# Turning the first two row tiles on TensorE, and a new order for every engine, in a two-layer linear-attention and SwiGLU kernel

## The chip, the cores and the metric

The kernel runs on one core of one Trainium2 chip. A core has five engines with instruction queues of their own: TensorE (PE), VectorE (DVE), ScalarE (ACT), GpSimd (POOL) and SyncE (SP), which here issues the DMA transfers. The metric is the device time of one execution, in microseconds (us).

## The reference

Two layers of two blocks each, with the same weights in both layers. The input is x with 2048 rows of 512 values; there are 32 heads of 16, and the hidden width of the gated block is 1792.

```python
def _A_ref(x, wqkv, wo):
    qkv = (x @ wqkv).reshape(B, S, 3, H, Dh).transpose(2, 0, 3, 1, 4)
    q, k, v = qkv[0], qkv[1], qkv[2]
    phi = lambda t: jnp.where(t > 0, t + 1, jnp.exp(t)) + 1e-6
    pq, pk = phi(q), phi(k)
    kv = jnp.einsum("bhsd,bhse->bhde", pk, v)
    z = jnp.einsum("bhsd->bhd", pk)
    num = jnp.einsum("bhqd,bhde->bhqe", pq, kv)
    den = jnp.einsum("bhqd,bhd->bhq", pq, z)[..., None] + 1e-6
    o = num / den
    return o.transpose(0, 2, 1, 3).reshape(B, S, D) @ wo

def _B_ref(x, w1, w3, w2):
    h = _silu(x @ w1) * (x @ w3)
    return h @ w2

x = x + _A_ref(_layernorm(x), wqkv, wo)
x = x + _B_ref(_layernorm(x), w1, w3, w2)
x = x + _A_ref(_layernorm(x), wqkv, wo)
x = x + _B_ref(_layernorm(x), w1, w3, w2)
```

## The kernel before, in words

**Precision.** A product of float32 matrices is made of float16 parts. Each operand is split into a high part (a rounded copy, by ACT, L834 for weights and L935 for normalised rows) and a low part (the rest, by DVE at L835 for weights, by POOL at L936 for rows), and `mm` (L945) runs three passes: high by high, high by low, low by high. So one product of a 128-row tile with a 512 x 512 weight is 4 x 3 = 12 matmuls of 512 columns.

**Tiles.** x is kept in SBUF as 16 row tiles of 128 rows. TensorE needs the rows of its operand turned (values on partitions): `ln_tile` (L930) normalises a tile (L922), splits it into the buffer `nat`, and has a transposing DMA transfer (L937) write the turned tile `xt`. The normalising needs mean and variance from DVE (L907, L908) and scale and offset from POOL (L915 to L919, `nb_all` last).

**Stages.** From 0 to about 13 us x and the weights of the keys come in, PE runs 32 matmuls on ones (`keep_busy`, named warm), and the largest weight is found: DVE's L787 and L803 give each partition's maximum, the small matmul `pm_k` (L806) spreads it, and DVE's L808 to L819 make the scale from it that the weight splits (L834) wait for. Then comes layer 0's attention: keys pk by row tile, their phi (L1337 to L1339), the products of keys and values kv (`gram`, L1364), then the queries, the output po and the adds to x (L1951). It is over at about 200 us, with the first MLP already mixed in. That MLP runs to about 577 us. It is written in a seven-product form (Strassen-Winograd) in half blocks of 256 columns: `mlp_group` (L2027) with DVE's block sums (L2022, L2023, L2053), and `mlp_out` (L2085; its matmuls are L2095, its adds L2144). Layer 1's attention, to about 760 us, has a seven-product form of its own, in which two row tiles are taken as a pair: `pair_rows` and `pair_turn` (L1564, L1569; sums L1573 to L1590 and the transposing transfer L1591), `products7` (L1595) with the banks ka to kc, qa to qc, whose results ACT and DVE combine (L1632, L1636), and `attention7` (L1640) with the pairs' loads `load7` (q_d and xt_d in DRAM), the phi of the queries (L1716), their division (L1730 to L1748), the products POOL rounds (L1758) and transposing transfers (L1767) ahead of the output po. Between keys and queries stand the folding of kv into the weights (L1794 to L1818). The second MLP runs to about 1140 us.

**What sets the order.** Nothing is left to a scheduler: `arrange` (L679) counts each engine's instructions in the order in which the program makes them, and pins them to the order that the table `ORDER` (L73) writes out, one list of numbers for each of PE, DVE, Activation, Pool and SP. An engine runs its list strictly in order, so an instruction that waits holds up all that stand behind it in the list. A DMA's place on SP's list sets when it can be issued.

**Names the prediction uses.** pk, kv, pq, po, kc, qa to qc, gt, ba to bc are PSUM banks by what is computed in them; `x_piece(t0, t1)` loads row tiles, `att_piece(1)` the four quarters of the keys' weights; `first_tile(t)` (L2339) makes the first turned tiles.

Of the kernel before, what the change touches and what calls it, by code (L numbers as in the profile page):

```python
# [495 lines left out]
def kernel(  # L496
# [1818 lines left out]
    def x_piece(t0, t1):  # L2315
        for t in range(t0, t1):
            nc.sync.dma_start(x_sb[:, t, :], x_rows[:, t, :])
# [120 lines left out]
```

## Time and profile before

| | |
|---|---|
| median of 3 runs | 1146.06 us (1145.27 to 1146.5) |
| the profiled execution's own time | 1146.37 us |
| its span in the profile | 1144.7 us |
| granted TensorE clock, mean | 0.999 |
| matmuls | 9108 |
| mean DMA rate | 143 GB/s |

The span runs from the first to the last instruction that the profiler recorded; what lies around it is part of the execution's time. A line of the trace has start and duration in us, the engine, the line of the source, the operation, out<-in and, in brackets, how long the engine was idle before it and what ended the idle time. Matmuls are pipelined: the recorded duration of one is longer than the distance to the next one's start.

### The profile page before, as it was taken

The page shows a single profiled execution, that of the slowest core. Times are in us where ns is not written, and L with a number is a line of the kernel's source. Part 1 is how long each engine was busy: PE and PEld are TensorE (multiplying, and loading weights), DVE is VectorE, ACT ScalarE, POOL GpSimd, SP SyncE. Part 2 cuts the span into 40 slices and gives each one's busy share as a digit, 9 for nine tenths or more (in the row PEclk, how much of TensorE's full clock was granted, in tenths as well). Part 3 has the DMA queues.
Part 4 walks back from the last instruction along what each step waited for, and adds up shares of the span by engine and source line. Part 5 has one row for each costly group of instructions (what it writes and reads, how often), then busy time and mean ns, then how long its engine had stood idle before and what let it go on. Part 6 is the DMA issues. An engine that isn't in the chain of part 4 may idle for free.

```text
span 1144.7 us, 22435 instructions
## 1 busy us (share of the span) xinstructions
PE 1126.6 (98%) x9108; PEld 887.6 (78%) x9108; DVE 853.8 (75%) x1468; ACT 656.7 (57%) x1099; POOL 422.4 (37%) x477
## 2 busy tenths in 40 slices
PE   8999999999999999999999999999999999999998
PEld 3445445888888888888885676578888888888887
DVE  6789878897888887889895478857855765455555
ACT  6687877765545545555577755676544335343432
POOL 5641796402001313334588315781153100302114
PEclk9999999999999999999999999999999999999999
DMA  9995855785662432251368955565256150202001
GB/s 271 298 268 181 211 119 114 209 243 109 244 230 97 153 148 102 85 179 65 79 169 196 248 169 127 97 152 148 70 113 257 70 207 1 84 19 93 11 19 56
DMA packets 173880, 163.46 MB, mean 143 GB/s; under 512 B 141648, under 2 KB 150096, under 8 KB 169168
## 3 DMA queue, kind: packets, MB, share of 16 engines
q1 hardware_dynamic: 173776, 162.03, 48.9%
q8 instruction: 71, 1.16, 0.4%
q14 instruction: 33, 0.27, 0.1%
HBM read 80.08 MB, written 47.32 MB: 111 GB/s over the span
## 4 chain that ended last, share of the span: by engine, by line
PE 86%; DVE 5%; ACT 3%; POOL 2%; DMA 2%; issue 1%; SPq 0%; DVEq 0%; POOLq 0%; ACTq 0%
PE bb L945 25%; PE po L2095 19%; PE bc L945 13%; PE ba L945 6%; PE gt L945 6%; PE po L945 4%; PE pk L945 3%; PE po L2115 3%; PE pq L945 3%; DMA arena<-arena 1%; PE kb L945 1%; PE qb L945 1%; DVE arena L869 1%; POOL arena L1590 1%; ACT arena L1632 1%
## 5 line engine op out<-in xcount | busy, mean ns | idle before, releaser
L945 PEld LDWEIGHTS <-arena 128*128 128x128 f16 x6648 | 645.9, 98 | 215.4 <-issue 10.4
L945 PE MATMUL bb<-arena 128*128 128x256 f16 x2688 | 351.2, 273 | 0.4 <-DMA arena<-arena 0.4
L2095 PE MATMUL po<-arena 128*128 128x256 f16 x2058 | 292.9, 273 | 0.7 <-DVE arena L2144 0.7
L2050 ACT ACTIVATE arena<-bb 128x512 f32<-128x512 f32 x196 | 115.6, 593 | 199.2 <-PE bb L945 168.2
L2095 PEld LDWEIGHTS <-arena 128*128 128x128 f16 x2058 | 201.3, 98 | 24.2 <-DVE arena L2144 1.0
L945 PE MATMUL bc<-arena 128*128 128x256 f16 x1344 | 179.7, 273 | 1.9 <-DVE arena L2053 1.9
L2053 DVE TENSOR_TENSOR arena<-arena,bc 128x512 f32<-128x512 f32 x112 | 76.6, 684 | 68.8 <-PE bc L945 33.7
L2011 DVE TENSOR_TENSOR arena<-arena 128x1280 f16<-128x1280 f32 (+1 forms) x90 | 105.4, 1174 | 28.5 <-ACT arena L2009 28.4
L2144 DVE SCALAR_TENSOR_TENSOR arena<-po,scalars,arena 128x256 f32<-128x256 f32 (+1 forms) x180 | 101.6, 585 | 30.8 <-PE po L2095 24.8
L2005 ACT ACTIVATE arena<-arena,scalars 128x512 f32<-128x512 f32 x112 | 74.5, 666 | 84.6 <-DVE arena L2053 70.7
L2009 ACT ACTIVATE arena<-arena 128x512 f16<-128x512 f32 (+1 forms) x112 | 100.6, 903 | 27.5 <-DVE arena L2006 9.7
L2006 DVE SCALAR_TENSOR_TENSOR arena<-arena,scalars 128x512 f32<-128x512 f32 x112 | 77.8, 695 | 38.1 <-ACT arena L2005 37.8
L945 PE MATMUL ba<-arena 128*128 128x256 f16 x672 | 92.3, 273 | 0.0
L945 PE MATMUL gt<-arena 128*128 128x512 f16 x384 | 89.4, 379 | 1.0 <-POOL arena L1652 1.0
L945 PE MATMUL po<-arena 128*128 128x512 f16 x384 | 86.5, 379 | 2.0 <-DMA arena<-arena 1.9
L2011 POOL TENSOR_TENSOR arena<-arena 128x512 f16<-128x512 f32 x22 | 28.2, 1280 | 125.8 <-ACT arena L2009 96.8
L2153 POOL TENSOR_TENSOR arena<-arena 128x512 f32<-128x512 f32 x27 | 37.8, 1402 | 94.5 <-DVE arena L2144 94.5
L2152 POOL TENSOR_TENSOR arena<-arena 128x512 f32<-128x512 f32 x27 | 36.8, 1362 | 65.0 <-DVE arena L2144 63.5
L869 DVE SCALAR_TENSOR_TENSOR arena<-arena,scalars 128x512 f16<-128x512 f32 (+2 forms) x74 | 59.8, 822 | 1.1 <-ACT arena L867 0.9
L922 ACT ACTIVATE arena<-arena,nb_all,rs_all 128x512 f32<-128x512 f32 x64 | 50.7, 805 | 14.2 <-POOL nb_all L919 8.9
L2021 POOL TENSOR_TENSOR arena<-arena 128x256 f32<-128x256 f32 x10 | 8.1, 814 | 133.1 <-DVE arena L2006 133.1
L867 ACT ACTIVATE arena<-arena,scalars 128x512 f16<-128x512 f32 (+2 forms) x74 | 52.1, 717 | 4.2 <-DVE scalars L819 1.8
(228 smaller groups left out, 1448.1 us busy)
## 6 DMA issues: line engine op xcount, KB each, us to landing
arena<-xb_d SPq DMA_DIRECT2D x12, 1792.0 KB, 7.1
xb_d<-arena SPq DMA_DIRECT2D x8, 1792.0 KB, 6.8
w_d<-arena SPq DMA_DIRECT2D x5, 1792.0 KB, 7.7
arena<-w_d SPq DMA_DIRECT2D x5, 1792.0 KB, 9.0
arena<-in_B_w_dram SPq DMA_DIRECT2D x8, 896.0 KB, 6.2
arena<-in_B_w_dram SPq DMA_DIRECT2D x28, 256.0 KB, 3.3
xt_d<-arena SPq DMA_DIRECT2D x8, 896.0 KB, 6.0
arena<-xt_d SPq DMA_DIRECT2D x8, 896.0 KB, 5.3
```

The source lines that it names most:

```text
L867: nc.scalar.activation(hi, src, AF.Copy, scale=scale)
L869: lambda: nc.vector.scalar_tensor_tensor(lo, src, scale, hi, OP.mult, OP.subtract)
L922: nc.scalar.activation(dst, x_sb[:, t, :], AF.Identity, scale=rs_all[:, t : t + 1], bias=nb_all[:, t : t + 1],)
L945: nc.tensor.matmul(dst, lhs(a, k), rhs(b, k), start=first and k == 0 and i == 0, stop=last and k == n - 1 and i == len(PASSES) - 1, skip_g ...
L2005: nc.scalar.activation(t, gate, AF.Silu, scale=info["u1"])
L2006: nc.vector.scalar_tensor_tensor(t, up, info["hid"], t, OP.mult, OP.mult)
L2009: nc.scalar.activation(hs[:, 0, lo:hi], t[:, lo:hi], AF.Copy)
L2011: engine.tensor_tensor(hs[:, 1, lo:hi], t[:, lo:hi], hs[:, 0, lo:hi], OP.subtract)
L2050: nc.scalar.activation(dst, bank_, AF.Copy)
L2053: nc.vector.tensor_tensor(dst, dst, bank_, OP.add)
L2095: nc.tensor.matmul(po[:, i * HALF : (i + 1) * HALF], hs[:, a, qx, cs], w2[:, b, qw, :], start=g == ends[0] and i + a + b == 0, stop=g == e ...
L2144: nc.vector.scalar_tensor_tensor(dst, src, cb, to, OP.mult, OP.add)
```

## The change

Tiles 0 and 1 are no longer turned by a transposing transfer. `first_tile` normalises them as before, and for the high and then the low part four TensorE matmuls with `ident16`, a float16 identity matrix that ACT copies out of `ident` at the start, write the turned part into a PSUM bank, from where one ACT copy moves it to `xt`. Tile 2 and all later ones still go by `ln_tile`. The program's order of loads is changed (tile 1 behind the keys' weights; a recorded handle in `x_piece` is not used by anything). PE has 16 instructions more, ACT 5 more, SP 2 fewer, DVE and POOL as many as before.

All five lists of `ORDER` are replaced. Since a list's numbers count the program's instructions, a number n of the old lists stands for the same instruction as n + 16 in PE's new list (from pm_k on), n + 5 in Activation's, n − 2 in SP's; in DVE's and Pool's it is the same.

```diff
 ORDER = {
     "PE": (
-        "0-56 69-80 57-68 93-104 81-83 90-92 84-89 117-128 114-116 108-110 141-152 105-107 "
...
-        "5365-5376 5341-5352 5419-5424 5377-5382 5395-5418 5431-5436 5425-5430 5389-5394 "
...
+        "0-20 22-31 34 21 35-37 32 38-48 33 49-72 85-96 73-84 109-120 100-102 97-99 106-108 "
...
+        "5375-5386 5339-5344 5399-5404 5435-5440 5387-5392 5357-5368 5393-5398 5411-5422 "
+        "5441-5452 5405-5410 5453-5476 5423-5434 5477-5572 5585-5596 5573-5584 5609-5620 "
...
     "DVE": (
-        "1 9-13 15 14 16-18 20-21 19 22 24 23 31 29 7 32 30 36 25 37 26-28 39-40 4 33 42 5 38 34 "
...
-        "317-318 294-296 298-300 308 302-305 349 335 321 307 306 350 311 320 319 339-340 310 322 "
...
-        "666 675 669 742 670 686 672 676 671 677-679 673 685 689 674 766 688 767 680 690 707 702 "
...
-        "959 964-965 985 968 972 970 984 973 971 969 986 988-989 992-995 991 990 987 997-998 "
...
-        "1028 1039-1040 1038 1031 1042-1046 1041 1047-1048 1057 1049-1050 1053-1054 1058 "
...
+        "294-296 298-299 770 300 302 304 308 303 289 305 349 335 321 307 306 350 319-320 311 "
...
+        "658 666 669 678 675-676 670 686 677 671 679 685 673 672 680 768 689 674 688 702 765 690 "
...
+        "980 962 964 966 968 965 985 969 972 984 970-971 973 986 992 988 993 989 994-995 990-991 "
...
+        "1030 1028 1027 1039-1040 1038 1031 1036 1042-1046 1041 1037 1049-1050 1047-1048 1057 "
...
     "Activation": (
-        "0-5 8-9 6-7 14 10 12 11 15 13 17 16 19 21 20 18 22-24 29 26-27 25 28 32 30 34-35 33 38 "
...
-        "752 722 760 751 731 759 724 732 768 727 725 733 726 761 728-730 741 737 767 736 743 739 "
...
+        "0-2 5-6 13 3-4 14 9-12 7-8 15 19 17 16 20 18 24 22 25 21 29 26 23 27-28 34 31 30 32-33 "
...
+        "724-725 720 727-728 757 756 764 736 765 737-738 729-730 766 731 746 772 747 732 748 741 "
...
     "Pool": (
...
-        "295 294 296-297 318-319 310 302 320 313 311 305 304 321 306-307 312 283 315 314 316-317 "
...
+        "272 274 265 303 293 247 273 248 276 278 277 252 249 253 255 292 279 254 267 302 266 "
...
     "SP": (
-        "0-2 4 3 5-7 25 8 11-12 9 21 18-19 22 20 23 10 26 30 36 24 27 17 28 48 31-32 13 34 54 42 "
...
-        "188 202 175 189 201 192 203-204 206 205 207 178 208-209 212 210-211 213-216 226 217 "
...
+        "0 5-6 1 3 2 4 7 9-10 20 19 17 16 23 18 21 8 24 28 22 25 15 34 26 52 29 36 40 53 32 30 27 "
...
+        "213-214 212 215 234 217-218 221-222 219 223 225-229 224 231-232 230 216 235 233 236 220 "
...
     ident = view(AT_UV + 2 * KB, F32, P)
     make_identity(nc, ident)
+    ident16 = view(AT_UV + 2 * KB + 512, F16, P)
+    nc.scalar.activation(ident16, ident, AF.Copy)
...
     def x_piece(t0, t1):
         for t in range(t0, t1):
-            nc.sync.dma_start(x_sb[:, t, :], x_rows[:, t, :])
+            last["t"] = nc.sync.dma_start(x_sb[:, t, :], x_rows[:, t, :])
...
-    x_piece(0, 2)
+    x_piece(0, 1)
     att_piece(1)
-    x_piece(2, 4)
+    x_piece(1, 4)
...
     def first_tile(t, engine=nc.gpsimd):
-        ready[0][t] = xk_ring.next(F16, 2 * NK, P)
-        ready[1][t] = ln_tile(t, ready[0][t], engine)
+        xt = ready[0][t] = xk_ring.next(F16, 2 * NK, P)
+        if t > 1:
+            ready[1][t] = ln_tile(t, xt, engine)
+            return
+        xn = f32()
+        normalise(xn, t)
+        nat = ready[1][t] = ring["nat"].next(F16, 2, D)
+
+        def turned(a):
+            turn = bank(f"turn{a}")
+            for k in range(NK):
+                at = slice(k * P, (k + 1) * P)
+                nc.tensor.matmul(turn[:, at], nat[:, a, at], ident16, start=True, stop=True)
+            flat = xt[:, a * NK : (a + 1) * NK, :].rearrange("p k n -> p (k n)")
+            nc.scalar.activation(flat, turn, AF.Copy)
+
+        nc.scalar.activation(nat[:, 0, :], xn, AF.Copy)
+        turned(0)
+        engine.tensor_tensor(nat[:, 1, :], xn, nat[:, 0, :], OP.subtract)
+        turned(1)
```

On SP's list the loads now run tile 0, 1, 2 of x, then the keys' weights, then the rest of x.

760 rows, old and new, of the table ORDER are left out of this document.

## The prediction

> **What bounds the kernel now.** I read the page's head first, to see which engine is full.
>
> ```profile
> span 1144.7 us, 22435 instructions
> PE 1126.6 (98%) x9108; PEld 887.6 (78%) x9108; DVE 853.8 (75%) x1468; ACT 656.7 (57%) x1099; POOL 422.4 (37%) x477
> PE 86%; DVE 5%; ACT 3%; POOL 2%; DMA 2%; issue 1%; SPq 0%; DVEq 0%; POOLq 0%; ACTq 0%
> ```
>
> TensorE (PE) is busy 1126.6 of 1144.7 us, so no new order can win more than the 18.1 us between them, and the ends before the first and after the last matmul come off that. The view of stretches, cut at the kernel's stages, tells where PE stands idle. The first figure of a row after the bounds is its length, the next PE's busy time.
>
> ```profile
> core 0: us, PE busy (x) PEld busy (x) DVE busy (x) ACT busy (x) POOL busy (x), PEclk, DMA share, GB/s
> 13.00:100.00 87.00, 86.06 (x399) 39.42 (x400) 72.49 (x145) 62.41 (x101) 41.05 (x89) 1.00 0.94 258
> 100.00:200.00 100.00, 97.60 (x531) 49.83 (x529) 84.84 (x167) 80.18 (x178) 69.54 (x69) 1.00 0.65 157
> 200.00:577.00 377.00, 376.04 (x3440) 336.14 (x3439) 318.62 (x545) 209.33 (x344) 104.94 (x106) 1.00 0.46 148
> 577.00:760.00 183.00, 176.05 (x1230) 117.95 (x1228) 129.25 (x216) 124.22 (x202) 105.60 (x107) 1.00 0.69 172
> 760.00:1140.00 380.00, 380.00 (x3476) 339.98 (x3475) 239.28 (x374) 174.29 (x270) 93.28 (x87) 1.00 0.27 88
> ```
>
> Idle are 0.94 + 2.40 + 0.96 + 6.95 + 0.00 = 11.25 us; layer 1's attention in pair form (577 to 760) has 6.95 of it, and the second MLP none. The list of what PE waited for (total, times, longest) names the pieces:
>
> ```profile
> PE bc L945 <- DVE arena L2053: 1.9, 1, 1.9
> PE po L945 <- DMA arena<-arena: 1.9, 1, 1.9
> PE qc L945 <- ACT arena L1632: 1.2, 1, 1.2
> PE pk L945 <- DMA arena<-arena: 1.2, 2, 1.0
> PE gt L945 <- POOL arena L1652: 1.0, 1, 1.0
> PE kc L945 <- DMA arena<-arena: 0.8, 1, 0.8
> PE po L2095 <- DVE arena L2144: 0.7, 1, 0.7
> PE qb L945 <- DVE arena L1636: 0.6, 1, 0.6
> PE pk L945 <- DVE arena L835: 0.6, 1, 0.6
> PE qa L945 <- DVE arena L1818: 0.6, 1, 0.6
> ```
>
> Most are single waits: a table that puts one operation earlier on the releasing engine removes one. A wait costs about 0.16 more than its idle, since a matmul of 512 columns is booked with 379 ns (0.38) and starts every 0.217, as (2.55 − 0.38)/10 from the row at 15.68 below shows.
>
> **The change, part by part. The start.** Its timeline (start, duration, last the idle and its releaser):
>
> ```profile
> 1.11 7.41 PE L2348 MATMUL warm<-ones 128*128 128x512 f16 x22 [1.11 <-DVE ones L708]
> 2.08 0.26 ACT masks.py:370 ACTIVATE mask<-mask 128x64 uint32<-128x64 uint32 x1
> 9.28 1.15 POOL L936 TENSOR_TENSOR arena<-arena 128x512 f16<-128x512 f32 x1 [0.21 <-ACT arena L935]
> 9.36 0.46 PE L806 MATMUL pm_k<-arena,scalars 128*128 128x128 f32 x2 [0.84 <-DVE scalars L803]
> 9.66 2.32 PE L2348 MATMUL warm<-ones 128*128 128x512 f16 x10
> 10.75 1.33 ACT L834 ACTIVATE arena<-arena,scalars 128x512 f16<-128x512 f32 x2 [1.54 <-DVE scalars L819]
> 11.64 1.23 SPq L937 DMA_TRANSPOSE arena<-arena  x1
> 12.98 2.11 PE L945 MATMUL pk<-arena 128*128 128x512 f16 x8 [1.00 <-DMA arena<-arena]
> 13.74 1.32 ACT L834 ACTIVATE arena<-arena,scalars 128x512 f16<-128x512 f32 x2
> 14.48 1.81 DVE L835 SCALAR_TENSOR_TENSOR arena<-arena,scalars 128x512 f16<-128x512 f32 x2 [1.47 <-ACT arena L834]
> 15.68 2.55 PE L945 MATMUL pk<-arena 128*128 128x512 f16 x11 [0.59 <-DVE arena L835]
> 17.09 0.67 ACT L1337 ACTIVATE arena<-pk,scalars 128x512 f32<-128x512 f32 x1
> ```
>
> *Removed*: two transposing transfers; tile 1's (issued at 11.64) releases pk at 12.98, and each kept SP's queue over 1.2 us, so tile 2's moves up. *Added*: 16 matmuls of 128 columns, four copies out of PSUM on ScalarE (ACT) and ident16's making.
>
> ```profile
> 108.82 2.03 PE kv L945 x36
> ```
>
> By this piece of the chain, 36 matmuls of 128 columns in 2.03 us, one takes 0.056, so 16 take 0.9 us. They lie in PE's idle time and between warm-ups, which only fill time, so I cost them at nothing. Without that cover they cost the 0.9.
>
> [...]
>
> Now what waits on what. In PE's new order pm_k stands behind tile 1's low-part transposes, so it starts when the low part (POOL L936, 10.43 before, some 0.07 later now) is done and turned, about 11.0 in place of 9.36. Queued behind it on PE are only ten warm-ups and the keys; DVE's scale and through it ACT's splits wait for it. From pm_k to the first weight split went 10.75 − 9.36 = 1.39; the splits (L834) start about 12.4. The new ACT table runs all four in a row, where before tile 2's normalising stood between the pairs: 12.4 + 4 × 0.66 = 15.05, as before (13.74 + 1.32 = 15.06). The last low part (L835) follows 0.8 behind, 15.85 in place of 14.48 + 1.81 = 16.29. Against that 0.44, tile 1's two PSUM copies, 0.67 each by the L1337 row, run after the splits and end near 16.4, which holds tile 1's keys about 0.15. Net gain: **0.3**. Bounds: −1.6 if both waits (1.0 and 0.6) vanish; +2.9 if all ACT's new work (4 × 0.67, and ident16's copy at about the 0.26 of the row at 2.08) goes ahead of the splits. Loads on SP's queue: tile 2 and the rest of x move ahead of the weights and put them back by less than pm_k now waits for the turning (1.6), so nothing; without that cover, one tile's issue and landing, under 1 us.
>
> **The waits later on**, each placed in the new tables against what it waited for:
>
> ```profile
> 741.16 2.61 SPq L1767 DMA_TRANSPOSE arena<-arena  x2
> 604.47 1.22 POOL L1652 COPY arena<-scalars 128x2 f16<-128x2 f16 x1
> 712.60 0.81 ACT L922 ACTIVATE arena<-arena,nb_all,rs_all 128x512 f32<-128x512 f32 x1 [2.17 <-POOL nb_all L1970]
> L2023 DVE TENSOR_TENSOR arena<-arena x39: 408/418/1484, 291.8 to 1119.4; 128x256 f32<-128x256 f32 x39
> ```
>
> - *po for the transposing transfer, 1.9.* VectorE's (DVE's) two adds of L1951 now stand behind L1716 of the last queries (positions 1036, 1037 behind 1031), so the work ahead of the transfers at 741.16 ends earlier; and PE's second twelve po matmuls (5423-5434) move behind 24 others (5453-5476), 12 × 0.217 = 2.6 us or more. Removed, 1.9 + 0.16 = 2.1.
> - *qc for L1632, 1.2.* The ACT copy queued behind L922, which waited 2.17 us for POOL; it now goes first (727 before 757). Removed, 1.4.
> - *gt for L1652, 1.0.* That POOL copy, held at 1.22 us, moves thirty places earlier. Removed, 1.2.
> - *po for L2144, 0.7.* It followed a 1.39 us instance of L2023 (row: median 0.418, most 1.484), which now comes after it. Removed, 0.8.
> - *qb for L1636*: five po matmuls move ahead: 0.6. *The second pk wait for a transfer*, 0.2: x comes earlier: 0.4.
> - *kc for a transpose, 0.8*: the ACT work ahead of it goes one place up, yet on SP's queue the load of q_d (row below) is moved from well behind to right behind it. I take half of 1.0: 0.5.
>
> Together 2.1 + 1.4 + 1.2 + 0.8 + 0.6 + 0.4 + 0.5 = **7.0** removed.
>
> ```profile
> 190.12 0.74 DVE L1951 SCALAR_TENSOR_TENSOR arena<-po,scalars,arena 128x512 f32<-128x512 f32 x1
> 681.86 1.22 DVE L1716 SCALAR_TENSOR_TENSOR arena<-arena 128x1024 f32<-128x1024 f32 x1
> arena<-q_d SPq DMA_DIRECT2D x1, 1792.0 KB, 10.8
> ```
>
> Given back, where the tables stand worse: bc's wait of 1.9 stays and gets another L1951 add ahead of its releaser, +0.7; qa's releaser L1818 changes places with its neighbour, +0.7; L1716 (1.22) goes ahead of the operation that pm waits for, of whose time PE's stock hides half, +0.6. **+2.0.** The queue also matters: q_d's load takes 10.8 us, and the last pair's transposes stand behind it, with 1.8 us to spare by the old times.
>
> Waits that only the new order makes have no row. From below: the bc, qa and kc waits left could go too, −4.3. From above: the new tables make as many as the old, 11.25 + PE's 0.16 for some fifteen waits, nearly all the gain. I take **+1.0**, near the low end, because the second MLP, the longest stage, shows that a stage can run with no idle and the releasers I could place have moved earlier more often than later.
>
> **The sum.** The profiled execution ran 1146.4 (its span 1144.7 and 1.7 around it), 0.3 above the median 1146.06. 1146.4 − 0.3 − 7.0 + 2.0 + 1.0 = 1142.1; less the 0.3, **1141.8**. A second way: if the pair stage came down to layer 0's attention (2.40 in 100 us, so 4.4 in 183), the gain would be 2.5, 1143.5.
>
> **Rivals.**
>
> *All of it goes.* Every idle of 11.25 vanishes: 1146.1 − 11.25 − 0.3 = 1134.5. The 0.00 row speaks for it; the places given back above speak against.
>
> *The start comes later.* pm_k behind the turning and ACT's copies ahead of the splits cost the 2.9 instead of gaining 0.3: 1141.8 + 3.2 = 1145.0. The row at 9.36 speaks for it: pm_k moves back 1.6 us in any case.
>
> *The clock drops in the start.* The 22 first warm-ups take 7.41/22 = 0.337 each, the next ten 0.232, so PE runs slower for a time. If a stretch without matmuls between turned tiles brought the slow phase back for the first 24 pk matmuls, that costs 24 × (0.337 − 0.232) = 2.5: 1144.3. Against it: 0.84 and 1.00 of idle before pm_k and pk leave the clock up today.
> [...]
>
> *Dealt anew, nothing won.* The tables remove the old waits and make as many: 1146.1. The given-back list shows that this happens.
>
> *The slower side: stretched VectorE work lands on the path.*
>
> ```profile
> L1924 DVE TENSOR_SCALAR den<-den x7: 168/292/2162, 112.2 to 186.3; 128x32 f32<-128x32 f32 x7
> ```
>
> Some DVE operations take 1 to 2 us more than their median (2.162 against 0.292, 1.484 against 0.418), each beside a long POOL operation. Which they meet depends on the tables; two of them stand ahead of waits today. If such a one, 1.4 us more on average, ends last ahead of matmuls in stages that have hardly any wait now, eight of them cost 11.2 on top of 1141.8, hence 1152 to 1153. Three undo the forecast's gain of 4.3, and from five on (7.0 against 4.3 + 2.3) the kernel is measurably slower. For it: 954 us of MLP work run full with nothing to gain. Against: PE's queue there holds many independent products.
>
> **How the numbers follow.** A measurement of this kernel can tell 0.2%, 2.3 us. Forecast 0.60 (1137, where the waits given 4.3 from below go as well and the rest holds, to 1146, where nothing is won), all goes 0.07, start later 0.08, clock 0.03, dealt anew 0.08, slower 0.14. Faster than 1143.8: 0.50 of the forecast's, the 0.07, 0.04 of the start's and clock's, 0.04 of the slower rival's mild cases, 0.65 in all. Slower than 1148.4: the 0.10 left of the slower rival, and 0.07 out of dealt anew and the forecast's tail, 0.17. Within: 0.18. The range starts at the forecast's 1137 and goes up to 1148.5, where the start's later case and dealt anew are in; all goes and most of the slower rival, some 0.2, are left out.
>
> **What would show it.** Right: pm_k near 11.0, first keys by 15, four L834 back to back; no po wait for a transpose near 742, no qc or gt wait; idle of 577 to 760 near 3; 760 to 1140 at 0 still. Wrong: a turning matmul over 0.2 us; a new wait over 1 us in an MLP stage; the chain passing through the load of q_d; bc's wait gone. The number is wrong if the pair stage's idle stays above 5, or the MLP stages show over 3.

## The result, and the profile after

| | before | changed |
|---|---|---|
| median | 1145.55 us (1145.27 to 1146.5, 6 runs) | 1139.47 us (1138.74 to 1140.93, 6 runs) |
| span of the profiled execution | 1144.7 us | 1138.1 us |
| ratio | | 0.9947, 95% interval 0.9934 to 0.9960 |

The change wins 6.1 us; forecast were 4.3. The page's head of the changed kernel:

```profile
span 1138.1 us, 22474 instructions
PE 1125.6 (99%) x9124; PEld 888.9 (78%) x9124; DVE 855.4 (75%) x1468; ACT 661.2 (58%) x1104; POOL 426.7 (37%) x477
PE 90%; DVE 4%; POOL 3%; ACT 2%; DMA 1%; issue 1%; SPq 0%; POOLq 0%; ACTq 0%; DVEq 0%
```

Of the 6.6 us of span that went, 5.6 are idle time (18.1 before, 12.5 now) and 1.0 is PE's busy time, although 16 matmuls came in. The stretches, cut at the points of the same work as before's (length first, then PE's busy time):

```profile
core 0: us, PE busy (x) PEld busy (x) DVE busy (x) ACT busy (x) POOL busy (x), PEclk, DMA share, GB/s
13.00:100.60 87.60, 86.26 (x404) 39.78 (x402) 72.82 (x148) 64.25 (x104) 40.45 (x87) 1.00 0.87 248
100.60:199.40 98.80, 97.54 (x532) 49.90 (x531) 84.54 (x168) 80.67 (x178) 71.06 (x69) 1.00 0.65 158
199.40:575.00 375.60, 375.43 (x3440) 336.38 (x3438) 320.46 (x541) 209.36 (x344) 108.52 (x107) 1.00 0.46 148
575.00:753.10 178.10, 175.41 (x1230) 117.95 (x1228) 128.44 (x218) 124.72 (x199) 105.25 (x105) 1.00 0.70 179
753.10:1133.50 380.40, 380.31 (x3477) 339.88 (x3475) 240.66 (x374) 174.81 (x271) 93.19 (x87) 1.00 0.28 88
```

The pair stage's idle fell from 6.95 to 2.69 (183.00 to 178.10 in length), layer 0's attention from 2.40 to 1.26, the first MLP from 0.96 to 0.17. The first stretch rose from 0.94 to 1.34, and the last MLP has 0.09. What PE still waits for:

```profile
PE turn L2352 <- POOL arena L2358: 2.0, 2, 1.4
PE po L945 <- DMA arena<-arena: 1.6, 2, 0.8
PE gt L945 <- DVE arena L1403: 1.3, 2, 0.7
PE bc L945 <- DVE arena L1951: 1.1, 1, 1.1
PE warm L2366 <- DVE ones L708: 1.1, 1, 1.1
PE qb L945 <- ACT arena L1632: 1.0, 1, 1.0
PE ba L945 <- DVE arena L2006: 0.2, 1, 0.2
```

Beside the first warm-up only po waits for the same releaser as before; qc, gt for POOL, kc, po for L2144, qa and pk are gone, gt for L1403 and qb for L1632 of ScalarE are new or grown. turn's 2.0 lie between the warm-ups, ahead of the first keys.

### The profile page after: what moved, and what is told of

Same layout as the page of the kernel before. It is cut to its first block, busy times and chain, and to the rows that moved or that the text cites. A ratio compares the mean times of both kernels' runs of the same rounds, so it can differ in the third digit from the quotient of the medians.

```text
span 1138.1 us, 22474 instructions
## 1 busy us (share of the span) xinstructions
PE 1125.6 (99%) x9124; PEld 888.9 (78%) x9124; DVE 855.4 (75%) x1468; ACT 661.2 (58%) x1104; POOL 426.7 (37%) x477
## 4 chain that ended last, share of the span: by engine, by line
PE 90%; DVE 4%; POOL 3%; ACT 2%; DMA 1%; issue 1%; SPq 0%; POOLq 0%; ACTq 0%; DVEq 0%
PE bb L945 24%; PE po L2095 20%; PE bc L945 12%; PE gt L945 7%; PE ba L945 6%; PE po L945 4%; PE po L2115 3%; PE pq L945 3%; PE pk L945 3%; PE kb L945 2%; PE qb L945 1%; PE kc L945 1%; PE qc L945 1%; DMA arena<-in_A_x_dram 1%; DVE arena L869 1%
## 5 line engine op out<-in xcount | busy, mean ns | idle before, releaser
L2095 PE MATMUL po<-arena 128*128 128x256 f16 x2058 | 288.1, 273 | 0.0
L2050 ACT ACTIVATE arena<-bb 128x512 f32<-128x512 f32 x196 | 115.4, 594 | 200.3 <-PE bb L945 165.5
L2053 DVE TENSOR_TENSOR arena<-arena,bc 128x512 f32<-128x512 f32 x112 | 76.6, 684 | 82.7 <-PE bc L945 48.6
L2144 DVE SCALAR_TENSOR_TENSOR arena<-po,scalars,arena 128x256 f32<-128x256 f32 (+1 forms) x180 | 101.2, 584 | 31.1 <-PE po L2095 21.8
L869 DVE SCALAR_TENSOR_TENSOR arena<-arena,scalars 128x512 f16<-128x512 f32 (+2 forms) x74 | 57.5, 792 | 2.5 <-ACT arena L867 2.4
L922 ACT ACTIVATE arena<-arena,nb_all,rs_all 128x512 f32<-128x512 f32 x64 | 50.6, 804 | 14.9 <-POOL nb_all L919 7.8
```

Source lines behind the costliest of these rows:

```text
L869: lambda: nc.vector.scalar_tensor_tensor(lo, src, scale, hi, OP.mult, OP.subtract)
L922: nc.scalar.activation(dst, x_sb[:, t, :], AF.Identity, scale=rs_all[:, t : t + 1], bias=nb_all[:, t : t + 1],)
L2050: nc.scalar.activation(dst, bank_, AF.Copy)
L2053: nc.vector.tensor_tensor(dst, dst, bank_, OP.add)
L2095: nc.tensor.matmul(po[:, i * HALF : (i + 1) * HALF], hs[:, a, qx, cs], w2[:, b, qw, :], start=g == ends[0] and i + a + b == 0, stop=g == e ...
L2144: nc.vector.scalar_tensor_tensor(dst, src, cb, to, OP.mult, OP.add)
```

## Where each kernel stands at equal work

In two traces the time at which PE has started the same number of matmul columns can be compared (warm-ups and turning left out). The table gives, in us, the start time less that of the kernel before at seven times of that kernel; negative is ahead. The kernels are those of the experiments below. A pair stage's gain is the column at 760 less that at 577.

| kernel | 20 | 185 | 195 | 577 | 716 | 760 | 1140 |
|---|---|---|---|---|---|---|---|
| changed | -0.36 | +0.15 | -0.65 | -2.00 | -7.20 | -6.86 | -6.51 |
| pair_only | -0.40 | +2.50 | +0.40 | +0.47 | -3.58 | -4.26 | -4.27 |
| start_only | -0.34 | -0.87 | +1.40 | +0.56 | -0.62 | +1.13 | +1.13 |
| no_turn | +2.16 | +1.25 | +0.46 | -0.89 | -5.01 | -5.67 | -5.64 |
| no_turn_late | +1.32 | +0.53 | -0.26 | -1.60 | -5.67 | -6.36 | -6.32 |
| four_back | +1.41 | +0.64 | -0.22 | -0.76 | -4.90 | -4.48 | -4.12 |
| five_forward | -0.31 | -1.45 | -2.50 | -3.58 | -9.68 | -7.50 | -6.93 |
| split_low | -0.42 | +1.33 | +0.54 | -0.82 | -6.05 | -6.11 | -5.74 |
| split_forward | -0.37 | -0.33 | -1.38 | -2.49 | -8.81 | -6.91 | -6.34 |
| bc_late | -0.17 | +1.63 | +1.40 | +1.25 | +1.28 | +1.27 | +1.27 |

The medians of the kernels from 1139.5 to 1141.7 have ratio intervals some 0.003 wide (3.4 us), so steps of one us are read from the traces, not from the medians. A trace is one execution of each kernel: what hangs on a late transfer in it can differ in another (pk waited 1.7 in pair_only and under 0.1 in before, with the same lists up to there).

## The experiments

**pair_only: the pair stage's order alone.** The lists of before up to 577 us and from 760 on, the new ones between; PE's differ from before's at 705 of 9091 places, ScalarE's at 120 of 1046. ScalarE's and DVE's at two places:

```diff
-"714 720 715 723 752 722 760 751 731 759 724"
+"716 714 719-720 715 722-723 752 751 759 731"
...
-"1030 1035 1029 1027 1036-1037 1028 1039-1040 1038"
+"1039-1040 1038 1031 1036 1042-1046"
```

> The kernel before, with the new lists' order in layer 1's pair stage alone (577 to 760 us); everything before and behind in the old order, tiles 0 and 1 turned by transfers. Theory A (the gain is a sum of single waits, each local to its stage): at equal work the stage gave 4.9 of the span's 6.5 between the two profiled runs, so 1145.6 - 4.9 = 1140.7, and the qc wait (1.2), the gt wait (1.0) and the kc wait (0.8) are gone while two po waits for transposes of about 0.8 stand near 740 and 750. Theory B (the new order pays only as a whole, because what one stage starts another needs): less than 2.5 of gain, above 1143.

Measured 1141.73, ratio 0.9953 (0.9936 to 0.9970), against the changed kernel's 0.9947. The stage gained 4.26 + 0.47 = 4.73, the changed kernel's 4.86: the stage's order pays by itself, and theory A holds for the stage as a whole. One wait didn't follow: kc still waits 1.1 us for a transfer, so that wait did not go by the order.

The turning took it away. In each of the nine kernels here that turn the first tiles on TensorE kc has no wait, start_only with before's order in this stage among them; in each of the five that use transfers (before, bc_late, pair_only, no_turn, no_turn_late) it waits 0.8 to 1.1. The transposing transfer that it waits for, of L1591, lands 5.9 to 6.1 us after its issue in those five and 4.4 to 5.0 in the nine; before's and start_only's, issued at 633.7 and 634.4:

```profile
DMA to landing us min/median/max: 5.9/5.9/5.9
DMA to landing us min/median/max: 4.4/4.4/4.4
```

Why two transposing transfers fewer at the start make one faster 620 us later is not shown. By the table the stage gains 5.20 up to 716 in the changed kernel and 4.05 in pair_only, 1.15 apart, and start_only, with before's order, gains 1.18, about kc's wait. By 760 that difference is gone again (4.86 and 4.73), in the waits of the stage's end.

This run shows a second thing. Up to 577 its lists are before's own, yet at 185 it was 2.50 behind:

```profile
PE pk L945 <- DMA arena<-arena: 2.0, 2, 1.7
PE bb L945 <- DMA arena<-arena: 1.6, 1, 1.6
```

In before the pk that waits 1.7 here waited under 0.1, and bb 0.4. The two transposing transfers landed 6.9 and 5.7 us after their issue, in before 5.5 and 4.6, so the same transfers came 1.4 and 1.1 us later in this execution. At 195 most of it was made good: bc's wait, 1.9 in before, is missing in this run. That wait comes when VectorE's chain ahead of it is done, whether PE arrives early or late.

**start_only: the turning with the start's order.** The changed program with the new lists up to 19.6 us and before's order behind, in its own numbers; where ScalarE's list parts:

```diff
-"7-8 15 19 17 16 20 18 24 22 25 21 29 26 23"
+"7-8 15 19 17 16 20 18 22 21 24 26 25 23 27-29"
```

> The turning by TensorE with the new order of the first 19.6 us, and the old order of all that follows. Theory A (the turning and the start's order are worth the 0.3 to 0.4 that the start shows, no more): 1145.2, and keys pk of tile 0 start near 13.6. Rival C (taking two transposing transfers off the queues pays later too, in the loads and transposes behind them): 1.5 or more of gain, 1144 or below. Rival D (the start costs, as in the prediction's later start): above 1147.

Measured 1147.0, ratio 0.9998 (0.9987 to 1.0010): nothing won. The start gained its 0.34, and 0.87 by 185, and then lost 2.27 at one place:

```profile
PE bc L945 <- DVE arena L2053: 2.5, 1, 2.5
PE po L945 <- DMA arena<-arena: 2.0, 1, 2.0
```

PE came 0.87 earlier to bc and waited 0.6 longer (2.5 for 1.9). Behind both waits the granted clock (PEclk, the third figure from a row's end) drops, to a mean of 0.55 in each stretch. Stretches of start_only:

```profile
191.40:195.00 3.60, 3.60 (x11) 1.28 (x10) 1.03 (x3) 3.59 (x9) 3.52 (x4) 0.55 0.67 153
744.50:748.00 3.50, 3.50 (x11) 1.24 (x10) 2.08 (x4) 1.71 (x3) 2.92 (x4) 0.55 0.64 119
```

Behind bc eight matmuls of 512 columns started every 0.43 in place of 0.217 us, 8 x 0.21 = 1.7. So bc's 0.6 of longer wait, of the 0.87 won ahead of it, came with a fall of the clock that cost 1.7. The po wait of 1.97 is only 0.06 longer than before's, which had no fall; the section on the hardware has both. Not every execution had both falls: the seven of twelve with a mean granted clock of 0.996 or 0.997 took 1146.9 to 1147.9, the five with 0.998 or 0.999 took 1145.2 to 1146.0. What rival C supposed shows at one place, kc's wait (1.0 with its 0.16), which this kernel no longer has; the second fall took it back.

**no_turn and no_turn_late: the new lists without the turning.** Tiles 0 and 1 by transposing transfers again (SP's list, numbers of before: 8 and 9), behind the loads of x's tiles 4 to 6 or, in the second, where before has them (the first transfer ahead of these loads, the second between them); SP's list in before's numbers, the changed kernel's first:

```diff
-"0 1 6 2 4 3 5 7 11 12 22 21 19 18 25"
+"0 1 6 2 4 3 5 7 11 12 22 21 8 9 19 18 25"
+"0 1 6 2 4 3 5 7 22 8 11 12 9 21 19 18 25"
```

> The new lists everywhere, but tiles 0 and 1 turned by the transposing transfers of before, put on SP's list behind the load of x's tile 6; ident16, the 16 matmuls and the 4 copies are left out. Theory A (the turning is worth nothing by itself; it even holds pm_k back by 1.6 us behind the low parts): pm_k near 9.6 in place of 11.06, the four splits from 11.0, keys from about 13, and the whole 0 to 1 us below the changed kernel: 1138.5 to 1139.5. Rival C (the turning by TensorE is what makes the start): keys no earlier than 14, 1 us or more above the changed kernel, 1140.5 or more.

> As no_turn, but x's tiles 4 to 6 are loaded behind the transposing transfers, as in the kernel before, in place of ahead of them. Theory K (in no_turn the transfer of tile 0 took 5.0 us from its issue at 9.44 to pk at 14.43, against 3.9 before, because the loads stood ahead of it in the DMA queues; turning by TensorE is what lets the loads go first): pk near 13.0 to 13.4, no slow matmuls behind it, the start within 0.5 of the changed kernel's, later waits for x's tiles near 25 to 30 as before (0.2 and 0.4); in all 1139.5 to 1140.3. Rival L (the transfer is late for another reason): pk at 14.4 again and 1141.

Measured 1140.95, ratio 0.9948 (0.9933 to 0.9964), and 1140.47, 0.9949 (0.9937 to 0.9962). Start of no_turn, and its stretch behind the wait:

```profile
9.44 3.77 SPq L937 DMA_TRANSPOSE arena<-arena  x2
11.01 2.56 ACT L834 ACTIVATE arena<-arena,scalars 128x512 f16<-128x512 f32 x4 [0.60 <-DVE scalars L819]
14.43 1.54 PE L945 MATMUL pk<-arena 128*128 128x512 f16 x5 [2.19 <-DMA arena<-arena]
```

```profile
15.50:18.90 3.40, 3.40 (x10) 1.16 (x8) 0.85 (x7) 0.00 (x0) 1.03 (x4) 0.53 0.93 171
```

The splits come 1.4 earlier than with the turning, as theory A had it, and it is no use: the first turned tile is there 5.0 us after its transfer was issued (14.43 - 9.44), PE waits 2.2, and the clock halves behind it. Rival C is right for the start: 2.5 behind the changed kernel at 20 us. With the loads behind the first transfer keys start at 13.60 and the clock holds, near what theory K gave; no_turn also issues the second transfer right behind the first, so that the loads alone made the 5.0 is not shown. no_turn_late then waits 1.5 for L835, since pm_k came at 10.61 in place of no_turn's 9.63. POOL's and PE's lists are the same in both; the keys' weights landed late, and VectorE's L787 and L803 ahead of pm_k with them:

```profile
8.31 1.95 DVE L787 TENSOR_REDUCE parts<-arena 128x1 f32<-128x512 f32 x3 [0.93 <-DMA arena<-in_A_wqkv_dram]
10.61 0.46 PE L806 MATMUL pm_k<-arena,scalars 128*128 128x128 f32 x2 [1.91 <-POOL arena L936]
```

(The view names POOL's L936 as the last to release pm_k; L803 ended at 10.46.) At the end little of either start is left, 0.9 and 0.2 of span. Nearly the whole gain of the tables stands without the turning; the turning's own share is at most some 1 us and not told apart by the medians.

**four_back: four single moves undone or turned round.**

```diff
 Activation
-"720 727-728 757 756"
+"720 728 757 727 756"
 DVE
-"675-676 670 686 677 671 679 685 673 672"
+"675 670 686 672 676-677 671 679 685 673"
-"298-299 770 300 302 304 308 303"
+"298-299 770 300 308 302 304 303"
 Pool
-"254 267 302 266"
+"254 267 266"
-"310 309 305 304"
+"310 309 302 305 304"
```

> The changed kernel with four single moves of its lists undone or turned round; each is read at its place. ACT's copy 727 (L1632) behind 757 (L922, which waits for POOL): a qc wait of about 1.75 comes back near 705 (copy ends 707.1 in place of 703.7, qc wants it at 705.4). DVE's 676 (L2144) behind 672 (L2023): a po wait of 1.2 near 467, 2.1 if L2023 is stretched to 1.4 again. POOL's 302 (L1652) behind 309: gt held at 601.95 until 602.25, 0.3, or 1.3 if the copy takes 1.2 again as it did before. DVE's L2053 of ba ahead of the L1951 add near 189: by theory A (the PSUM bank that a tile gets is dealt by the order, so bc waits for whichever of the two frees a bank first) the releaser becomes L2053 and the wait stays at 1.1 within 0.1; by rival E (bc's bank is fixed, it is po's) the wait grows by 0.7 to 1.8. Sum by theory A: 1139.5 + 3.3 to 5.2 = 1142.8 to 1144.7; if the waits are absorbed by work behind them (rival F), under 1141.

Measured 1141.74, ratio 0.9956 (0.9941 to 0.9971).

```profile
PE qc L945 <- ACT arena L1632: 1.6, 1, 1.6
PE bc L945 <- DVE arena L2053: 1.1, 1, 1.1
PE po L945 <- DVE arena L1951: 0.7, 1, 0.7
PE po L2095 <- DVE arena L2144: 0.6, 1, 0.6
```

qc came back with 1.6 + 0.16 = 1.75 as worked out, po for L2144 with 0.7, below the 1.2 expected (that L2023 was not stretched); gt for L1652 shows no wait where 0.3 was expected. But the changed kernel's qb wait of 1.0 is gone in exchange: both belong to ScalarE's queue behind L922, and the move of L1632 is worth 0.6 net (1.75 - 1.15 by the distance of the matmuls), not 1.4. bc's releaser turned from L1951 to L2053 with the wait unchanged, as theory A said. In the built programs that bc's PSUM bank is ba's in before and po's in the changed kernel; 267 of 464 PSUM tiles have another bank. The bank that a tile gets is dealt by the order.

**five_forward: five waits of the changed kernel attacked.**

```diff
 PE
-"31 34 21 35-37 32 38-48"
+"31 34 38 21 35-37 32 39-48"
 DVE
-"43 55 60 44 67"
+"43 55 44 60 67"
-"62 104 59 66"
+"62 59 104 66"
-"294-296 298-299 770 300 302 304"
+"294-296 302 298-299 770 300 304"
 Activation
-"757 756 764 736 765"
+"736 757 756 764 765"
```

> The changed kernel with five single moves against waits that its trace still shows: pm_k ahead of the last warm-up and three low-part turns (10.65 in place of 11.06, 0.4); DVE's L1403 ahead of two row statistics that wait for loads of x (gt at 27.85 and 41.60: 0.87 and 0.6); DVE's first L1951 add (302) ahead of the stretched L1924 (bc at 189.6: 1.3); ACT's L1632 (736) ahead of the L922 that waits for POOL (qb at 708.5: 1.15). Theory A (single waits add up): 4.3 below the changed kernel, 1135.2. Theory G (a wait that VectorE's chain of work sets comes at its own time, and what PE gains ahead of it is lost there: the two po waits near 737 and 747 take back the last 1.15): about 3.2, 1136.3, with longer po waits. Rival F (the work moved back makes new waits of the same size): no better than 1138.7.

Measured 1140.55, ratio 0.9952 (0.9938 to 0.9967): no better than the change, rival F in the total. The trace says where it went. gt's waits went (1.6), bc's too, for a new wait of bb:

```profile
PE po L945 <- DMA arena<-arena: 1.8, 3, 0.8
PE qc L945 <- DVE arena L1636: 0.9, 1, 0.9
PE bb L945 <- ACT arena L2050: 0.9, 1, 0.9
PE qb L945 <- ACT arena L1632: 0.5, 1, 0.5
```

pm_k, 0.4 earlier (10.67), won nothing: at 20 us it stands at -0.31 to -0.36, as the ten warm-ups and the turns stand between pm_k and the keys. At 716 it was 9.68 ahead, 2.5 better than the changed kernel (7.20); at 760 7.50 to 6.86. The last queries took it back.

**split_low and split_forward: the transposes at the end of the pair stage.** POOL's last-pair-but-one L1758 in two halves, so that the first tile is turned earlier; the second also has the four later moves of five_forward.

```diff
-nc.gpsimd.tensor_tensor(nat[:, lo:hi, 1, :], row(r), nat[:, lo:hi, 0, :], OP.subtract)
+if p != 6: nc.gpsimd.tensor_tensor(nat[:, lo:hi, 1, :], row(r), nat[:, lo:hi, 0, :], OP.subtract)
 for i in range(lo, hi):
+    if p == 6: nc.gpsimd.tensor_tensor(nat[:, i, 1, :], r[:, i].rearrange("p h n -> p (h n)"), nat[:, i, 0, :], OP.subtract)
```

> The changed kernel, with POOL's L1758 of the last pair but one (1024 columns, 2.13 us at 731.1) done as two operations of 512, so that the first tile's transposing transfer is issued 1.05 earlier. Theory G (the end of the pair stage is set by the chain of the last pair on VectorE, ScalarE and POOL, so time won ahead of it only lengthens the next wait): the po wait of 0.98 at 736.6 goes, the one of 0.99 at 746.7 grows to about 1.9, and the time stays within 0.3 of the changed kernel's. Rival A (single waits add up): 1.0 less, 1138.5.

> split_low's division together with the four later moves of five_forward (not pm_k's). Theory G: PE reaches the last pairs some 2 us earlier and loses it there again; the span stays within 1.0 of the changed kernel's 1138.1, and po waits near 735 and 745 sum to 2 us or more. Rival A: 3.0 to 3.5 below the changed kernel, 1136.

Measured 1140.2, ratio 0.9949 (0.9936 to 0.9961), and 1140.85, 0.9958 (0.9944 to 0.9972). Waits of split_low:

```profile
PE gt L945 <- DVE arena L1403: 2.6, 2, 2.0
PE bb L945 <- DMA arena<-arena: 0.8, 1, 0.8
PE po L945 <- DMA arena<-arena: 0.3, 1, 0.3
```

po's 1.6 fell to 0.3, and bb, which waits for the transposing transfer of x's rows, has 0.8 now: 0.8 of the 1.3 came back, but not as a longer po wait, as theory G said. split_forward led the changed kernel by 1.61 at 716 (8.81 to 7.20) and by 0.05 at 760. Theory G holds in its main claim: at the end of the pair stage PE waits for chains through VectorE, ScalarE, POOL and a transfer, and what PE wins ahead of them lengthens or makes waits there. No version tried beats the changed kernel.

**bc_late: a longer wait ahead of bc in before.** `"294-296 298-300 308 302-305"` became `"294-296 303 298-300 308 302 304-305"` on DVE's list.

> The kernel before with one DVE operation (303, an L869 weight split of 0.75 to 1.26 us) moved ahead of L1924, so that the bc wait near 190 grows from 2.10 to between 2.85 and 3.36. Theory H (PE's clock falls to half after about 2.1 to 2.7 us without matmuls, as it did behind the waits of 2.14, 2.35 and 2.69 of the runs so far, and costs 8 matmuls x 0.21 = 1.7): eight to sixteen matmuls at double spacing behind the wait, 2.5 to 3.0 slower in all, 1148.6 to 1149.1. [...] Rival J (the waits behind absorb it): 1146.1.

Measured 1148.12, ratio 1.0021 (1.0009 to 1.0032); 1.27 in the trace. Inconclusive on the clock: a late transfer held PE up 1.6 just before, bc's wait became 1.7 in place of 2.7 to 3.2, and the clock held.

**clock_dose, 2 and 3: PE's waits and the clock behind them.** Copies of ones onto themselves on ScalarE ahead of four L2050 of the second MLP of the changed kernel, 16, 22, 28 and 36, then 12, 14, 27, 12, then 9, 11, 22, 9:

```diff
 pair(1, nxt, None, second)
+for _ in range(16 + 22 + 28 + 36):
+    nc.scalar.activation(ones16, ones16, AF.Copy)
```

> The changed kernel with 16, 22, 28 and 36 idle ScalarE copies (ones onto themselves, some 0.2 us each) ahead of four L2050 of the second MLP, near 820, 896, 976 and 1058, a stage in which PE has no wait; PE will wait there for growing times (each block less some 2 to 3 us of slack: about 1, 2, 3 and 5). Theory H (a wait from about 2.0 us on lets the granted clock fall to about half for some 3.3 us, at 1.7 us of extra time each): granted clock about 0.55 in the stretch behind each wait of 2.0 or more, none behind shorter ones; the extra time of each place is the wait plus 1.7. [...] Rival M (the half clock in three runs so far has nothing to do with the waits): no stretch of 0.55, or one away from the four places.

> As clock_dose, with 12, 14, 27 and 12 copies at the four places in place of 16, 22, 28 and 36. In clock_dose the waits were 3.7, 5.4, 3.6 and 10.2 and one copy took 0.34, so they should now be 2.3, 2.7, 3.25 and 2.0 (extra time to the next matmul; the recorded idle is 0.16 less). Theory H: half clock behind all four, 10.2 of waits and 4 x 1.6 = 6.4 behind them, 16.6 above the changed kernel, 1156.1. [...]

> As clock_dose2, with 9, 11, 22 and 9 copies: waits of 1.3, 1.7, 1.55 and 1.0. By theory H and by rival I alike no half clock, 5.5 above the changed kernel, 1145.0; a stretch near 0.55 behind one of them would put the bound below 1.7.

Measured 1168.74, 1152.16 and 1145.84. One copy took 0.34 (the 0.2 was the author's estimate), so the waits of the first run, 3.7, 5.4, 3.6 and 10.2, were all above theory H's 2.0 and none below it was tried; the clock fell behind all four, and each place cost 1.3 to 1.9 beyond its wait. In the second the waits were 2.3, 2.7, 3.25 and 2.0 as worked out, and in the profiled execution only the third brought the clock down:

```profile
822.00:826.00 4.00, 4.00 (x37) 3.59 (x37) 3.01 (x5) 2.13 (x4) 1.52 (x2) 1.00 1.19 273
900.00:904.00 4.00, 4.00 (x37) 3.59 (x37) 0.25 (x1) 1.68 (x2) 0.00 (x0) 1.00 0.02 4
985.20:989.20 4.00, 3.99 (x24) 2.96 (x24) 0.00 (x0) 1.50 (x2) 0.00 (x0) 0.63 0.73 303
1069.70:1073.70 4.00, 4.00 (x37) 3.58 (x37) 2.29 (x3) 1.69 (x2) 0.00 (x0) 1.00 0.00 0
```

Its other executions took 1151.84 to 1153.91, at a mean clock of 0.997, against the profiled one's 1149.73 at 0.999; the median of 1152.16 lies 3.9 below theory H's 1156.1. The third run's profiled execution, with waits up to 1.7, had no stretch at half clock. Rival I, named in its expectation, supposed that only longer waits than theory H's bring a fall; no run shows where such a bound would lie.

## Why the prediction was right, and which steps of it failed

**The start: right in each step.** Rows of the changed kernel:

```profile
10.84 0.39 PE L2352 MATMUL turn<-arena 128*128 128x128 f16 x4
11.06 0.44 PE L806 MATMUL pm_k<-arena,scalars 128*128 128x128 f32 x2
12.43 2.56 ACT L834 ACTIVATE arena<-arena,scalars 128x512 f16<-128x512 f32 x4 [1.22 <-DVE scalars L819]
13.19 2.74 DVE L835 SCALAR_TENSOR_TENSOR arena<-arena,scalars 128x512 f16<-128x512 f32 x4
13.50 0.22 PE L2352 MATMUL turn<-arena 128*128 128x128 f16 x1
13.55 4.74 PE L945 MATMUL pk<-arena 128*128 128x512 f16 x21
14.90 1.06 ACT L2354 ACTIVATE arena<-turn 128x512 f16<-128x512 f32 x2
```

pm_k at 11.06 (worked out 11.0), splits at 12.43 (12.4), the last low part done at 15.93 (15.85), 0.36 ahead at 20 us (0.3). A turning matmul took (0.39 - 0.22)/3 = 0.057 from start to start, the row's 0.056, and one by itself is recorded with 0.22. Only the copies were dearer in the estimate (0.67) than in fact (1.06 for two). What the step missed lies behind it: start_only shows that the 0.34 does not reach the end. And the start can fail in the same program: four_back's has the changed kernel's lists, but there the turns waited 1.86 + 0.60 us, the clock fell to 0.50 from 10.91 to 14.32, and keys began at 15.37 in place of 13.55.

**The waits removed: 7.0 predicted, right in their places, wrong in three sizes.** gt for POOL and po for L2144 went and stayed away (1.2 and 0.8). qc went, but "it now goes first" looked at one copy only; the next L1632 (736) still stands behind L922 and holds qb up 1.0. po "removed, 2.1" failed: two po waits, 0.8 each, end the same chain of VectorE, ScalarE, POOL and a transposing transfer, whose last pair the reordering did not shorten.

```profile
733.25 2.61 SPq L1767 DMA_TRANSPOSE arena<-arena  x2
736.56 1.68 PE L945 MATMUL po<-arena 128*128 128x512 f16 x7 [0.82 <-DMA arena<-arena]
```

kc, taken at half for a place on ScalarE's and SP's queues, went whole and for another reason: it goes in every kernel with the turning, start_only with the old order included, and in none without it, as its transfer lands 4.4 to 5.0 us after issue in place of 6.0. That this term came near was luck.

**The waits given back, +2.0: the step that failed.** None came. "bc's wait of 1.9 stays and gets another L1951 add ahead of its releaser" took the releaser for fixed. With the new order bc has another bank, is released by the first L1951 and waits 1.1: -0.8 in place of +0.7; four_back turned the releaser back with one move. "qa's releaser changes places with its neighbour" looked two places to each side; the wait went, as L1730 of 1.22 us, which stood between the second and the third L1818, now stands ahead of all four:

```profile
677.55 1.22 DVE L1730 SCALAR_TENSOR_TENSOR arena<-arena 128x1024 f32<-128x1024 f32 x1
678.96 0.75 DVE L1818 SCALAR_TENSOR_TENSOR arena<-pm,scalars,arena 128x512 f16<-128x512 f32 x1 [0.19 <-ACT arena L1817]
682.10 1.36 DVE L1818 SCALAR_TENSOR_TENSOR arena<-pm,scalars,arena 128x512 f16<-128x512 f32 x2
```

pm's +0.6 did not show either. Against the term two of the three places moved the other way, some -1.5 for bc and qa together.

**The new waits, +1.0: too low.** gt for L1403, 0.87 and 0.80 by the distance of the matmuls, comes from row statistics that wait for loads of x and hold VectorE's queue up; with qb's 1.15 and three below 0.35 (0.9 together) it makes 3.7. On the other side some ten waits of before below 0.6, which I had left out, went too. The errors largely cancelled in the sum, which is luck: 4.3 for 6.1.

**The rivals.** The second MLP shows 0.09 of idle, and VectorE's stretched operations reached PE nowhere in it: the slower rival did not occur. (The 954 us of MLP work that spoke for it are 757, 377 and 380, by the stretches.) The later start and the falling clock did not occur in the changed kernel's profiled execution. The clock did in four_back, whose start is the same, and its keys began 1.8 later; in two of the changed kernel's six executions the mean granted clock is 0.998 and the time the longest, 1140.26 and 1140.93, which one fall would make (half of 3.41 us is 0.0015 of the span), though no trace of them shows where. It also fell in start_only and no_turn. A fall cost 1.3 to 1.9 where 2.5 was worked out. "All of it goes" did not hold: 5.55 us of idle are left.

## What to carry to other kernels

A wait that another engine's chain sets comes at its own time: PE's gains ahead of it were lost there (start_only's 0.87 ahead of bc; split_forward's lead of 1.61 at 716, 0.05 at 760), so look for the waits that end last, and count a gain only from behind the last of them. A reordering changes more than the neighbours on one list: it dealt PSUM banks anew here (267 of 464 tiles), and one wait removed can leave the next instruction of the same queue to wait (qc's 1.2 went, and qb waits 1.0); follow the queue to its end before a term is entered. Keep PE's waits short for what comes behind them too: behind waits of 1.97 and 2.52 (start_only) and 2.19 (no_turn), and behind two close ones of 1.86 and 0.60 (four_back), the granted clock fell to 0.50, and a fall cost 1.3 to 1.9 us; behind 2.14 and 2.52 in clock_dose2 it held. A wait that goes need not have gone by the change that was meant for it: kc's, of 0.8 to 1.1 us, shows in all five kernels without the turning, with the old order and with the new.

## What the runs showed of the hardware

Behind PE waits the granted clock fell to 0.50, for 3.41 us at both places of start_only, for longer behind the longest wait of clock_dose (0.50 through the 3.80 us from 1086.80 on), and in the MLP stage each fall cost 1.3 to 1.9 us beyond the wait. The length of the wait does not sort them: recorded idle of 1.97 and 2.52 in start_only and of 2.19 in no_turn brought a fall, 2.14 and 2.52 in clock_dose2 did not.

The times at which the granted clock changes lie whole multiples of 3.4133 us apart in the traces of three kernels: the two falls of start_only, at 191.26 and 744.22, are 552.96 = 162 x 3.4133 apart; in before the record of the clock starts at 6.19 and turns to 0.50 behind the last matmul at 1142.82, 1136.64 = 333 x 3.4133 later, in the changed kernel at 5.18 and 1138.40, 1133.23 = 332 x 3.4133. The table has stretches of that length, and PE's idle in each beside the clock in the next:

| run and stretch | PE idle in it | clock in the next stretch |
|---|---|---|
| clock_dose2 981.36 to 984.77 | 2.64 | 0.50 |
| four_back 7.50 to 10.91 (two waits, 1.86 and 0.60) | 2.46 | 0.50 |
| clock_dose 991.77 to 995.18 (of a wait of 3.43) | 2.22 | 0.50 |
| no_turn 11.84 to 15.25 | 2.19 | 0.50 |
| start_only 187.85 to 191.26 | 2.11 | 0.50 |
| start_only 740.81 to 744.22 | 1.97 | 0.50 |
| clock_dose2 896.03 to 899.44 (of a wait of 2.52) | 1.99 | 1.00 |
| split_low 26.35 to 29.76 | 1.95 | 1.00 |
| before 187.09 to 190.50 | 1.94 | 1.00 |
| clock_dose2 817.52 to 820.93 (of a wait of 2.14) | 1.10 | 1.00 |
| before 740.05 to 743.46 (of a wait of 1.91) | 0.95 | 1.00 |

Three of these stretches as the view by stretches gives them, start_only's second with the one behind it and clock_dose2's of 1.99; idle is the first figure less the second:

```profile
740.81:744.22 3.41, 1.44 (x7) 0.51 (x6) 3.31 (x7) 0.00 (x0) 3.41 (x3) 1.00 0.74 142
744.22:747.63 3.41, 3.41 (x10) 1.21 (x8) 2.36 (x4) 1.34 (x3) 2.83 (x4) 0.50 0.59 112
896.03:899.44 3.41, 1.42 (x14) 1.13 (x12) 3.17 (x6) 3.10 (x11) 1.26 (x1) 1.00 0.00 0
```

In these rows 1.97 us of idle and 2.11 to 2.64 were followed by half clock; 0.95 to 1.95 and 1.99 were not. po's wait of 1.97 lay whole in one stretch in start_only; its 1.91 in before was cut into 0.95 and 0.96, and the clock held. That the idle in one such stretch goes with a fall, and not the length of the wait, is the author's reading of these rows; no run moved a wait against the stretches with all else alike.

The transposing transfer of tile 0 let PE go on 3.9 us after its issue in before (12.98 - 9.10), 4.2 in no_turn_late (13.60 - 9.44) and 5.0 in no_turn (14.43 - 9.44), where three more loads of x stood ahead of it and the second transfer was issued right behind it. And with identical lists up to there, pk waited under 0.1 us in before and 1.7 in pair_only for the same transfer, which landed 5.5 and 6.9 us after its issue.
